# Three of eight 1/z factors brought to xT's layout by DMA, and a planner constant raised from 22 to 24

## The chip, the cores and the metric

The kernel runs on one core of one Trainium2 chip. The metric is the device time of one execution in microseconds, taken as the median of three runs. A core has five engines with queues of their own: TensorE (PE; its weight loads stand apart as PEld), VectorE (DVE), ScalarE (ACT), GpSimd (POOL) and SyncE (SP, which here only issues DMAs). Each works through its queue strictly in the order in which its instructions were written; a letter q behind an engine's name in a row means its sequencer, which issues DMAs and waits.

## The reference, cut to what matters

The program is masked attention followed by two feed-forward blocks. Only the attention's last line is touched by the change: each row of `attn` is divided by its own sum z.

```python
scores = np.where(mask, scale * np.matmul(q, k.transpose(0, 1, 3, 2)), -1e9)   # mask: equal 6-bit hash buckets
scores = scores - np.max(scores, axis=-1, keepdims=True)
attn = np.exp(scores)
attn = attn / (np.sum(attn, axis=-1, keepdims=True) + 1e-09)
attn_out = np.matmul(attn, v)                          # (2, 8, 768, 64)
x = attn_out.transpose(0, 2, 1, 3).reshape(2, 768, 512)
# gated block: h = relu(x @ w_in), spatial mixing by w_spatial, @ w_out
# second block: layer norm, relu(xn @ w_ch1) @ w_ch2, added to its input
```

## The kernel before

**Tiles.** There are 2 batches x 8 heads x 6 tiles of 128 queries, 96 tiles in all. A name such as `x_1_6_1_0` is tile x of batch 1, head 6, group 1 (of two groups of three tiles), tile 0 in the group. For each tile PE computes the scores `sc` (128 queries x 768 keys), DVE takes the masked minimum into `x`, ACT the exponential with its row sum into `z_sum`, PE turns `x` by 6 transposes into `pt` (PSUM, two halves), ACT and DVE copy the halves to `e`, and PE multiplies `e` by `vv` into `po`, once for each head. ACT and DVE copy `po` into `xT`, where a partition is a channel (64 channels for each of two heads of a pair) and a column is a query. `sc` has two PSUM buffers, and `pt`, `po`, `pm` and `pz` share a ring of four.

**Division by z.** The factors 1/z stand with queries on the partitions, `xT` has the queries in its columns. For each of the eight head pairs (`b`, `r`) `summed` adds 1e-9 and takes the reciprocal (`zr`, 128 x 12), one tile after the pair's last `weighted`; `normalized`, three tiles after it, lets POOL widen `zr` to 128 x 384 twice (`zw`), PE transpose each into PSUM (`pz`, three 128 x 128 transposes each), and DVE multiply `xT` by it in two halves. `attn_step` calls both.

**What comes after.** The gated block of batch 0 runs on PE between the tiles of batch 1's attention (`pv`, `pg`, `py`). Batch 1's own gated block begins when attention ends: `x_split` splits `xT` into high and low parts (`act_x`), and for it all four pairs of batch 1 must be divided. Then come the second block's matmuls (`pc`, `p`, `acc`). Weights come as 64-bit words (`f_v`, `f_u`, `f_w` in the rows, `f64_...` in the program) through ACT's DMA queue and are converted by ACT, DVE and POOL; the rest of the loads and all stores are issued by SP.

**What sets the order.** All calls are recorded as jobs. `Plan.run` gives each a start from its own table of costs and due times, twelve rounds of it are made, the best one by that table is kept, and the instructions of each engine are written in the order of these starts. A job that isn't PE's may not start more than `EARLY` before its due time `late[j]` (line 180 and `opened` in `run`), so `EARLY` moves work on every engine but PE directly, and on PE through what is ready:

```python
return max(when[i], bulk, late[j] - self.EARLY) if late and not j.soon else max(when[i], bulk)
```

Of the kernel before, what the change touches and what calls it, by code (L numbers as in the profile page):

```python
# [9 lines left out]
F32 = mybir.dt.float32  # L10
# [4 lines left out]
ALU = mybir.AluOpType  # L15
# [3 lines left out]
P = 128  # L19
# [150 lines left out]
class Plan:  # L170
# [6 lines left out]
    RUN = 6  # L177
    NEAR = 1.5
    LOOK = 55
    EARLY = 22.0  # L180
    BULK = 14.0
    ROUNDS = 12
    HOP = {"PE": 0.15, "ACT": 0.06, "DVE": 0.06, "POOL": 0.06, "SP": 0.05}
# [115 lines left out]
    def run(self, late=None):  # L299
# [20 lines left out]
        def opened(j):  # L320
# [3 lines left out]
            bulk = self.BULK if j.engine == "ACT" and j.bytes > 200000 else 0.0  # L324
            return max(when[i], bulk, late[j] - self.EARLY) if late and not j.soon else max(when[i], bulk)

# [185 lines left out]
def attn_moe_kernel(ctx: ExitStack, tc: tile.TileContext, qT, kT, v, proj, w_in, w_spT, b_sp, w_out, g_ln, w1, w2, out):  # L512
    fixed = ctx.enter_context(tc.tile_pool(name="fixed", bufs=1))
    ident = fixed.tile([P, P], F32, name="ident")
    make_identity(tc.nc, ident)
    nc = plan = Plan(tc)
    B, H, D, S = qT.shape
# [8 lines left out]
    NQT = S // P  # L526
# [25 lines left out]
    GW = GRP * P  # L552
    NG = NQT // GRP
    KC = S // 2
# [89 lines left out]
    dram = Pool(plan, "dram", space=bass.MemoryType.DRAM)  # L644
# [34 lines left out]
    xT = {}  # L679
    z_sum = {}  # L680

    pairs = {}
# [65 lines left out]
    NT = len(order)  # L748
# [74 lines left out]
    def head_prep3(b, h):  # L823
        vv = ap.tile([P, NKT, D], F32, tag="vv", name=f"vv_{b}_{h}", bufs=2)
        nc.sync.dma_start(out=vv, in_=v[b, :, h])
        heads[b, h]["vv"] = vv

    def group_prep(b, h, g):
        groups[b, h, g] = {"qs": passes_of("q", b, h, slice(g * GW, (g + 1) * GW))}

    def scores(b, h, g, j):
        jm = f"{b}_{h}_{g}_{j}"
        ks, qs = heads[b, h]["ks"], groups[b, h, g]["qs"]
        qsl = slice(j * P, (j + 1) * P)
        sc = ps_s.tile([P, 1024], F32, tag="sc", name=f"sc_{jm}")[:, :S]
        for csl in (slice(0, 512), slice(512, S)):
            for i, rows in enumerate((P, MR)):
                nc.tensor.matmul(
                    sc[:, csl], qs[:rows, i, qsl], ks[:rows, i, csl], start=(i == 0), stop=(i == 1)
                )  # L840
        tiles[b, h, g, j] = {"sc": sc}

    def masked_max(b, h, g, j):

        jm = f"{b}_{h}_{g}_{j}"
        t = tiles[b, h, g, j]
        x = ap.tile([P, S], F32, tag="x", name=f"x_{jm}", bufs=XB)
        nb = ap.tile([P, 1], F32, tag="nb", name=f"nb_{jm}", bufs=4)
        nc.vector.tensor_scalar(
            x,  # L850
            t["sc"],
            MASKED,
            FMAX,
            op0=ALU.min,
            op1=ALU.min,
            accum_out=nb,
        )
        t["x"], t["nb"], t["max"] = x, nb, plan.jobs[-1]
        if (b, h, g, j) == (0, 0, 0, 0):
            pair_split(0, 0, first=True)  # L860

    def exps(b, h, g, j):
        t, n = tiles[b, h, g, j], g * GRP + j
        nc.scalar.activation(
            t["x"], t["x"], AF.Exp, bias=t["nb"], scale=-1.0, accum_out=z_sum[b][:, n, h : h + 1]
        )

    def transposes(b, h, g, j):
        jm = f"{b}_{h}_{g}_{j}"
        t, gr = tiles[b, h, g, j], groups[b, h, g]  # L870
        if j == 0:
            gr["e"] = ap.tile([P, NKT, GW], F32, tag="e", name=f"e_{b}_{h}_{g}", bufs=EB)
        qsl = slice(j * P, (j + 1) * P)
        for c in range(2):
            pt = ps_b.tile([P, 3, P], F32, tag="b", name=f"pt_{jm}_{c}")
            for i in range(3):
                kt = c * 3 + i
                nc.tensor.transpose(pt[:, i, :], t["x"][:, kt * P : (kt + 1) * P], ident)
            e = gr["e"][:, c * 3 : c * 3 + 3, qsl]
            if c == 0 or (b == 0 and (g * GRP + j) % 2):  # L880
                nc.scalar.activation(e, pt, AF.Copy)
            else:
                nc.vector.tensor_copy(e, pt)

    def weighted(b, h):
        po = ps_b.tile([P, GW], F32, tag="b", name=f"po_{b}_{h}")
        for kt in range(NKT):
            for g in range(NG):
                nc.tensor.matmul(
                    po[g * D : (g + 1) * D],  # L890
                    heads[b, h]["vv"][:, kt],
                    groups[b, h, g]["e"][:, kt],
                    start=(kt == 0),
                    stop=(kt == NKT - 1),
                )
        own = slice(h % 2 * D, (h % 2 + 1) * D)
        nc.scalar.activation(xT[b][own, h // 2, 0:GW], po[0:D], AF.Copy)
        nc.vector.tensor_copy(xT[b][own, h // 2, GW:S], po[D:P])
        for g in range(NG):
            groups.pop((b, h, g))  # L900

    def summed(b, r):

        zr = ap.tile([P, NQT, 2], F32, tag="zr", name=f"zr_{b}_{r}")
        nc.vector.tensor_scalar(zr, z_sum[b][:, :, 2 * r : 2 * r + 2], 1e-9, None, op0=ALU.add)
        nc.vector.reciprocal(zr, zr)
        pairs[b, r]["zr"] = zr

    def normalized(b, r):

        zr = pairs[b, r]["zr"]
        for c in range(2):
            zw = ap.tile([P, 6, D], F32, tag="zw", name=f"zw_{b}_{r}_{c}", bufs=2)
            zc = zr[:, c * 3 : c * 3 + 3, :].rearrange("p a (h o) -> p (a h) o", o=1)
            nc.gpsimd.tensor_scalar(zw, zc.to_broadcast([P, 6, D]), 1.0, 0.0, op0=ALU.mult, op1=ALU.add)
            pz = ps_b.tile([P, 3, P], F32, tag="b", name=f"pz_{b}_{r}_{c}")
            for i in range(3):
                nc.tensor.transpose(pz[:, i, :], zw[:, 2 * i : 2 * i + 2].rearrange("p h d -> p (h d)"), ident)
            xs = xT[b][:, r, c * KC : (c + 1) * KC]
            nc.vector.tensor_tensor(xs, pz.rearrange("p a n -> p (a n)"), xs, op=ALU.mult)  # L920

    def attn_step(i):

        if 0 <= i < NT:
            transposes(*order[i])
        if 0 <= i + 2 < NT:
            b, h, g, j = order[i + 2]
            if (h, g, j) == (0, 0, 0):
                xT[b] = mp.tile([P, KFT, S], F32, tag="xT", name=f"xT_{b}")
                z_sum[b] = mp.tile([P, NQT, H], F32, tag="z_sum", name=f"z_sum_{b}")  # L930
            scores(*order[i + 2])
        if 0 <= i + 1 < NT:
            masked_max(*order[i + 1])
            exps(*order[i + 1])
        if 0 <= i - PO < NT and order[i - PO][2:] == (NG - 1, GRP - 1):
            weighted(*order[i - PO][:2])
        for late, e in ((1, summed), (3, normalized)):
            n = i - PO - late
            if 0 <= n < NT and order[n][1] % 2 == 1 and order[n][2:] == (NG - 1, GRP - 1):
                e(order[n][0], order[n][1] // 2)  # L940
        n = i + 1 + QA
        if GRP < n < NT and order[n][3] == 0:
            group_prep(*order[n][:3])
        n = i + NTH
        if NTH <= n < NT and order[n][2:] == (1, 0):
            head_prep3(*order[n][:2])
# [9 lines left out]
    for n0 in range(0, NT, 2 * NTH):  # L956
        b, h = order[n0][:2]
# [227 lines left out]
    ap = Pool(plan, "ap", 2, till=1)  # L1185
    conv0 = pools["conv"] = Pool(plan, "conv0", CB0, till=1)
    ps_s = Pool(plan, "ps_s", 2, space=PSUM, till=1)
    ps_b = Pool(plan, "ps_b", 4, space=PSUM, till=1)
# [18 lines left out]
    for n, f in enumerate(KEPT):  # L1207
        d = {}
# [21 lines left out]
    for i in range(-1 - QA, NT + PO + 3):  # L1230
        attn_step(i)
        for e in pair_steps.get(i, ()):
            e()
        if i == 2:
            nc.sync.dma_start(out=b_sb, in_=b_sp.rearrange("(n p) -> p n", p=P))
        plan.soon = True
        for e in conv_steps.get(i, ()):
            plan.behind = pools.get("abs", pairs[0, 1]["loaded"]) if e.__name__ in ("stage", "kept_stage") else None
            e()
        plan.soon, plan.behind = False, None  # L1240
        if i == M0:
            m0 = moe1(0, ps_b, "b")
        if m0 is not None:
            while n0 < (i - M0 + 1) * 24 / (NT - M0):
                next(m0, None)
                n0 += 1
# [362 lines left out]
    late = []  # L1609
    for n, (b, rs_of) in enumerate(runs):  # L1610
        for m, r in enumerate(rs_of):
# [25 lines left out]
            both = (2 * r, 2 * r + 1)  # L1637
# [43 lines left out]
```

## Time and profile before

| | |
|---|---|
| median of 3 runs | 646.39 us (645.65 to 646.80) |
| the profiled execution's own time | 645.79 us |
| its span, first to last instruction | 643.6 us |
| PE busy | 634.8 us, 99% of the span |
| DVE busy | 500.4 us, 78% |
| ACT busy | 327.7 us, 51% |
| POOL busy | 189.6 us, 29% |
| granted TensorE clock, mean | 0.999 of full speed |

Durations in the rows are of single instructions; on PE they overlap, so that a PE instruction's duration is longer than the distance to the next one's start. What an instruction takes out of PE's time is read from the chain of waits, which gives each piece only the time up to the next one.

### The profile page before, as it was taken

The numbers are of one execution on the slowest core, as the hardware profiler recorded it, in microseconds if no ns is written. First come the engines' busy times: TensorE is split into PE (matmuls) and PEld (weight loads), VectorE is DVE, ScalarE is ACT, GpSimd is POOL, SyncE is SP. The second block draws the span as 40 slices with busy tenths as digits, with TensorE's granted clock in tenths as the row PEclk, the third lists the DMA queues.
The fourth block names the chain that finished last, engine by engine and source line by source line (L and its number), as shares of the span: only waits on it lengthen the run. The fifth ranks groups of instructions, "written<-read, shape, count | busy, mean of one in ns | idle before, by whom it ended". The sixth has DMA issues, their size and how long they took to land.

```text
span 643.6 us, 10095 instructions
## 1 busy us (share of the span) xinstructions
PE 634.8 (99%) x3506; PEld 520.3 (81%) x3506; DVE 500.4 (78%) x998; ACT 327.7 (51%) x650; POOL 189.6 (29%) x186
## 2 busy tenths in 40 slices
PE   7999999999999999999999999999999999999997
PEld 5777767777787777877888888899999899898896
DVE  6789878797888686886799544699998887969555
ACT  7888877885565655643555323554323333333110
POOL 2142433244554633131343200122122324142200
PEclk9999999999999999999999999999999999999999
DMA  6776676667767877774653240421262626382623
GB/s 153 195 206 155 181 181 154 183 145 240 204 181 243 235 195 212 228 264 176 231 167 145 73 148 17 147 86 46 99 231 114 234 92 223 105 279 74 218 88 143
DMA packets 64738, 107.68 MB, mean 167 GB/s; under 512 B 7008, under 2 KB 33328, under 8 KB 64432
## 3 DMA queue, kind: packets, MB, share of 16 engines
q1 hardware_dynamic: 43232, 67.58, 36.0%
q10 hardware_dynamic: 21456, 39.46, 18.5%
q8 instruction: 28, 0.46, 0.3%
q14 instruction: 22, 0.18, 0.1%
HBM read 63.31 MB, written 24.90 MB: 137 GB/s over the span
## 4 chain that ended last, share of the span: by engine, by line
PE 94%; DMA 2%; DVE 2%; issue 1%; SPq 0%; POOL 0%; ACTq 0%; DVEq 0%; POOLq 0%
PE acc L502 20%; PE p L502 14%; PE pv L502 10%; PE sc L502 10%; PE pt L502 10%; PE po L502 9%; PE pg L502 7%; PE pc L502 5%; PE py L502 5%; DMA qs<-q 2%; PE pm L502 1%; PE pz L502 1%; PE ptr_g L502 1%; PE px_c L502 1%; DMA pj<-in_proj 1%
## 5 line engine op out<-in xcount | busy, mean ns | idle before, releaser
L502 PE MATMUL acc<-w,ch 128*128 128x512 f32 x576 | 142.9, 393 | 0.0
L502 PEld LDWEIGHTS acc<-w,ch 128*128 128x128 f32 x576 | 107.3, 188 | 18.9
L502 ACT ACTIVATE x<-x,nb 128x768 f32<-128x768 f32 x96 | 89.7, 936 | 31.3 <-DVE x L502 26.4
L502 DVE TENSOR_SCALAR_CACHE_REDUCE x<-sc 128x768 f32<-128x768 f32 x96 | 90.9, 951 | 6.8 <-PE sc L502 3.7
L502 PE MATMUL sc<-ks,qs 128*128 128x512 f32 (+3 forms) x384 | 93.8, 363 | 1.9 <-DVE x L502 1.2
L502 POOL TENSOR_TENSOR f64c_w<-f_w,f64c_w 128x512 f32<-128x512 f32 x32 | 44.1, 1380 | 152.9 <-issue 81.8
L502 PE MATMUL pt<-ident,x 128*128 128x128 f32 x576 | 81.3, 274 | 0.3 <-DVE xT L502 0.3
L502 PEld LDWEIGHTS pt<-ident,x 128*128 128x128 f32 x576 | 66.5, 140 | 14.9 <-issue 2.4
L502 PEld LDWEIGHTS sc<-ks,qs 128*128 128x128 f32 (+1 forms) x384 | 62.9, 190 | 13.9 <-issue 2.2
L502 PE MATMUL po<-e,vv 128*64 128x384 f32 x384 | 65.5, 490 | 0.0
L502 ACT ACTIVATE ch<-u 128x384 fp32r<-128x384 f32 x48 | 25.2, 525 | 79.1 <-DVE u L502 67.0
L502 ACT ACTIVATE e<-pt 128x384 f32<-128x384 f32 x120 | 55.0, 485 | 18.6 <-PE pt L502 18.1
L502 DVE TENSOR_TENSOR u<-p,u 128x384 f32<-128x384 f32 x84 | 45.4, 552 | 20.5 <-PE p L502 20.0
L502 PEld LDWEIGHTS po<-e,vv 128*64 128x64 f32 x384 | 26.1, 137 | 31.2 <-issue 29.8
L502 PE MATMUL p<-t,w 128*128 128x384 f32 x252 | 50.0, 337 | 0.0
L502 PE MATMUL p<-xh,w 128*128 128x384 f32 x252 | 48.8, 338 | 0.0
L502 DVE COPY e<-pt 128x384 f32<-128x384 f32 x72 | 39.7, 553 | 9.6 <-PE pt L502 9.0
L502 PEld LDWEIGHTS p<-t,w 128*128 128x128 f32 x252 | 44.9, 188 | 2.3
L502 PEld LDWEIGHTS p<-xh,w 128*128 128x128 f32 x252 | 44.6, 188 | 2.2 <-DVE u L502 0.3
L502 POOL TENSOR_TENSOR w<-f64c_w,w 128x512 fp32r<-128x512 f32 (+1 forms) x28 | 35.2, 1259 | 37.8 <-ACT w L502 15.0
L502 DVE TENSOR_SCALAR f64c_w<-f64c_w 128x512 f32<-128x512 f32 x64 | 30.8, 480 | 18.5 <-ACT f64c_w L502 15.8
L502 PE MATMUL pg<-vn,w_sp 128*128 128x512 f32 x180 | 43.6, 396 | 0.0
(155 smaller groups left out, 1018.5 us busy)
## 6 DMA issues: line engine op xcount, KB each, us to landing
f_w<-in_w ACTq DMA_DIRECT2D x32, 512.0 KB
ots<-y_dram SPq DMA_DIRECT2D x12, 768.0 KB
ks<-k SPq DMA_DIRECT2D x45, 192.0 KB
y_dram<-ots SPq DMA_DIRECT2D x30, 256.0 KB
qs<-q SPq DMA_DIRECT2D x30, 192.0 KB
wst_sp<-in_w_spT SPq DMA_DIRECT2D x12, 384.0 KB
vv<-in_v SPq DMA_DIRECT2D x16, 192.0 KB
qs<-q SPq DMA_DIRECT2D x30, 96.0 KB
```

The source lines that it names most:

```text
L502: res = getattr(getattr(nc, engine[j.engine]), op)(*map(live, args), **{k: live(x) for k, x in kw.items()})
```

## The change

Three pairs of batch 1 (`r` = 0, 1, 2) take another way. `zr` is laid out as 128 x (2 heads x 6 tiles), so that one transpose gives 12 rows of 128 queries (`pz`, 12 x 128); DVE copies these to `zt`, SP stores `zt` to `zd` in DRAM (6 KB), and two DMAs read it back, each row broadcast to 64 partitions, as `zb` (128 x 768). DVE multiplies `xT` by `zb` in one instruction. `normalized` for these pairs is called eight tiles behind, not three. The other five pairs keep PE's way; their `zw` is now one tile for both halves, in one buffer (shared with `zb`) where there were two, and POOL fills it with four instructions of 128 x 3 x 64 where there were two of 128 x 384. For all eight pairs the 1e-9 is added in two instructions (one for each head). `EARLY` goes from 22 to 24.

```diff
-    EARLY = 22.0
+    EARLY = 24.0
...
     def summed(b, r):
-        zr = ap.tile([P, NQT, 2], F32, tag="zr", name=f"zr_{b}_{r}")
-        nc.vector.tensor_scalar(zr, z_sum[b][:, :, 2 * r : 2 * r + 2], 1e-9, None, op0=ALU.add)
+        zr = ap.tile([P, 2, NQT], F32, tag="zr", name=f"zr_{b}_{r}")
+        for h in range(2):
+            nc.vector.tensor_scalar(zr[:, h], z_sum[b][:, :, 2 * r + h], 1e-9, None, op0=ALU.add)
         nc.vector.reciprocal(zr, zr)
         pairs[b, r]["zr"] = zr
+        if b == 0 or r == H // 2 - 1:
+            return
+        rows = 2 * NQT
+        pz = ps_b.tile([P, GW], F32, tag="b", name=f"pz_{b}_{r}")
+        nc.tensor.transpose(pz[:rows, :P], zr.rearrange("p h a -> p (h a)"), ident)
+        zt = ap.tile([rows, P], F32, tag="zt", name=f"zt_{b}_{r}", bufs=1)
+        nc.vector.tensor_copy(zt, pz[:rows, :P])
+        zd = dram.tile([2, 1, S], F32, tag=f"zd_{b}_{r}", name=f"zd_{b}_{r}")
+        nc.sync.dma_start(out=zd.rearrange("h o (a q) -> (h o a) q", a=NQT), in_=zt)
+        zb = ap.tile([P, S], F32, tag="zw", name=f"zb_{b}_{r}", bufs=1)
+        for h in range(2):
+            nc.sync.dma_start(out=zb[h * D : (h + 1) * D], in_=zd[h].to_broadcast([D, S]))
+        pairs[b, r]["zb"] = zb
     def normalized(b, r):
+        if "zb" in pairs[b, r]:
+            nc.vector.tensor_tensor(xT[b][:, r], pairs[b, r]["zb"], xT[b][:, r], op=ALU.mult)
+            return
         zr = pairs[b, r]["zr"]
+        both = ap.tile([P, S], F32, tag="zw", name=f"zw_{b}_{r}", bufs=1)
         for c in range(2):
-            zw = ap.tile([P, 6, D], F32, tag="zw", name=f"zw_{b}_{r}_{c}", bufs=2)
-            zc = zr[:, c * 3 : c * 3 + 3, :].rearrange("p a (h o) -> p (a h) o", o=1)
-            nc.gpsimd.tensor_scalar(zw, zc.to_broadcast([P, 6, D]), 1.0, 0.0, op0=ALU.mult, op1=ALU.add)
+            zw = both[:, c * KC : (c + 1) * KC].rearrange("p (a h d) -> p a h d", a=3, h=2)
+            for h in range(2):
+                zc = zr[:, h, c * 3 : c * 3 + 3].rearrange("p (a o) -> p a o", o=1)
+                nc.gpsimd.tensor_scalar(zw[:, :, h], zc.to_broadcast([P, 3, D]), 1.0, 0.0, op0=ALU.mult, op1=ALU.add)
...
-        for late, e in ((1, summed), (3, normalized)):
+        for late, e in ((1, summed), (3, normalized), (8, normalized)):
             n = i - PO - late
+            if late > 1 and (late == 8) != (n > NT // 2 and n < NT - 1):
+                continue
```

The order of the instructions changes in many places on each engine. Three of them matter below. The first is on PE, at the pair `r` = 1 of batch 1. Before, behind the first scores of head 5:

```order
L502 MATMUL pt_1_4_1_1_1_2707<-ident_58,x_1_4_1_1_2655 128x128 x3
L502 MATMUL sc_1_5_0_0_2711<-ks_1_5_0_2412,qs_1_5_0_2518 128x512 x2
L502 MATMUL sc_1_5_0_0_2711<-ks_1_5_0_2412,qs_1_5_0_2518 128x256 x2
L502 MATMUL pz_1_1_0_2719<-ident_58,zw_1_1_0_2613 128x128 x3
L502 MATMUL pz_1_1_1_2726<-ident_58,zw_1_1_1_2616 128x128 x3
L502 MATMUL pv_0_5_0_2731<-w_u_0_1170,act_x0_5_2424 128x512 x12
```

After, the pair's only transpose stands some ten rows earlier, between two tiles of head 4:

```order
L502 MATMUL pt_1_4_0_2_1_2636<-ident_58,x_1_4_0_2_2518 128x128 x3
L502 MATMUL sc_1_4_1_1_2640<-ks_1_4_0_2221,qs_1_4_384_2396 128x512 x2
L502 MATMUL sc_1_4_1_1_2640<-ks_1_4_0_2221,qs_1_4_384_2396 128x256 x2
L502 MATMUL pz_1_1_2650<-ident_58,zr_1_1_2528 12x128
L502 MATMUL pt_1_4_1_0_0_2652<-ident_58,x_1_4_1_0_2579 128x128 x3
L502 MATMUL pt_1_4_1_0_1_2658<-ident_58,x_1_4_1_0_2579 128x128 x3
```

Six transposes have become one; it reads `zr` itself, with no `zw` between. The second place is on ACT, in the first heads of batch 0, where the first piece of the weights (`f64_v_0`) is loaded and then read by `f64c_v_0`. Before:

```order
L502 ACTIVATE e_0_1_0_382<-pt_0_1_0_0_0_361 128x3x128
L502 DMA f64_v_0_387<-in_w_in 128x1024
L502 ACTIVATE x_0_1_0_2_377,z_sum_0_218<-x_0_1_0_2_377,nb_0_1_0_2_376 128x768
L502 ACTIVATE e_0_1_0_382<-pt_0_1_0_1_0_391 128x3x128
L502 ACTIVATE e_0_1_0_382<-pt_0_1_0_1_1_398 128x3x128
L502 ACTIVATE x_0_1_1_0_423,z_sum_0_218<-x_0_1_1_0_423,nb_0_1_1_0_422 128x768
L502 ACTIVATE x_0_1_1_1_431,z_sum_0_218<-x_0_1_1_1_431,nb_0_1_1_1_430 128x768
L502 ACTIVATE f64c_v_0_435<-f64_v_0_387 128x512
```

After:

```order
L502 ACTIVATE e_0_1_0_381<-pt_0_1_0_0_0_369 128x3x128
L502 ACTIVATE x_0_1_0_2_364,z_sum_0_215<-x_0_1_0_2_364,nb_0_1_0_2_363 128x768
L502 ACTIVATE e_0_1_0_381<-pt_0_1_0_1_0_389 128x3x128
L502 ACTIVATE e_0_1_0_381<-pt_0_1_0_1_1_393 128x3x128
L502 DMA f64_v_0_412<-in_w_in 128x1024
L502 ACTIVATE x_0_1_1_0_410,z_sum_0_215<-x_0_1_1_0_410,nb_0_1_1_0_409 128x768
L502 ACTIVATE x_0_1_1_1_430,z_sum_0_215<-x_0_1_1_1_430,nb_0_1_1_1_429 128x768
L502 ACTIVATE f64c_v_0_438<-f64_v_0_412 128x512
```

The load's issue has moved three instructions back, its reader has stayed in its place. The third place is near the end of attention, on SP, after the change (`wst_sp0_4` and `wst_sp0_5` are pieces of w_spatial, `qs_1_7_384` the queries of the last head's second group, `y_0_1` a result tile of batch 0):

```order
L502 DMA wst_sp0_4_3146<-in_w_spT 128x6x128
L502 DMA zb_1_0_3151<-zd_1_0_2321 64x768 x2
L502 DMA y_dram_3035<-y_0_1_3180 128x512
L502 DMA zb_1_1_3221<-zd_1_1_2897 64x768
L502 DMA qs_1_7_384_3236<-q2_1_3_2583 64x2x384
L502 DMA qs_1_7_384_3236<-q2_1_3_2583 64x384
L502 DMA qs_1_7_384_3236<-m_1_3_2786 12x384
L502 DMA zb_1_1_3221<-zd_1_1_2897 64x768
L502 DMA zd_1_2_3269<-zt_1_2_3214 12x128
L502 DMA wst_sp0_5_3302<-in_w_spT 128x6x128
L502 DMA zb_1_2_3322<-zd_1_2_3269 64x768 x2
```

and on DVE at the same place, where the first of these products stands ahead of the scores of head 6:

```order
L502 COPY e_1_6_0_3053<-pt_1_6_0_2_1_3182 128x3x128
L502 TENSOR_TENSOR xT_1_1862<-zb_1_0_3151,xT_1_1862 128x768
L502 COPY zt_1_2_3214<-pz_1_2_3196 12x128
L502 TENSOR_SCALAR x_1_6_1_1_3217,nb_1_6_1_1_3216<-sc_1_6_1_1_3186 128x768
L502 COPY e_1_6_1_3208<-pt_1_6_1_0_1_3204 128x3x128
L502 TENSOR_SCALAR x_1_6_1_2_3240,nb_1_6_1_2_3239<-sc_1_6_1_2_3210 128x768
```

The reads of `zb` stand late, close ahead of the products that take them, and all three pairs are divided within this stretch. `zb` has one buffer, so the read of `zb_1_1` waits for the product of `zb_1_0`, and `qs_1_7_384` stands behind it on SP.

## Rows read from the trace of the kernel before

**Rows 1.** The page's busy times: engine, us, share of the span, instructions.

```profile
PE 634.8 (99%) x3506; PEld 520.3 (81%) x3506; DVE 500.4 (78%) x998; ACT 327.7 (51%) x650; POOL 189.6 (29%) x186
```

**Rows 2.** What PE waited for: us in total, times, longest.

```profile
PE warm L502 <- POOL above L502: 1.4, 1, 1.4
PE pm L502 <- DVE qs L502: 1.3, 1, 1.3
PE sc L502 <- DVE x L502: 1.2, 2, 0.9
PE sc L502 <- DMA qs<-q: 0.5, 1, 0.5
PE pt L502 <- DVE xT L502: 0.3, 1, 0.3
PE sc L502 <- PE pt L502: 0.2, 1, 0.2
```

**Rows 3.** Windows, last stretch: length, then busy us of each engine, clock, DMA.

```profile
620.00:644.00 24.00, 19.82 (x93) 16.82 (x91) 12.76 (x22) 1.58 (x3) 0.00 (x0) 0.97 0.35 132
```

**Rows 4.** Instructions that touch pz: ns min/median/max, first and last start us.

```profile
L502 PE MATMUL pz<-ident,zw x48: 269/273/330, 46.6 to 302.6; 128*128 128x128 f32 x48
L502 DVE TENSOR_TENSOR xT<-pz,xT x16: 547/552/558, 47.9 to 303.7; 128x384 f32<-128x384 f32 x16
```

**Rows 5.** Chain of waits near the pair (1, 2): start us, us up to the next piece.

```profile
264.40 0.66 PE pz L502 x6
265.06 2.77 PE py L502 x12
```

**Rows 6.** Instructions that touch zw and zr: ns min/median/max, first and last start us.

```profile
L502 POOL TENSOR_SCALAR zw<-zr x16: 510/512/941, 36.3 to 294.6; 128x384 f32<-128x384 f32 x16
L502 DVE TENSOR_SCALAR zr<-z_sum x8: 161/169/1323, 34.1 to 293.6; 128x12 f32<-128x12 f32 x8
```

**Rows 7.** Timeline of DVE in the start: start us, us, [idle before].

```profile
9.49 0.55 DVE L502 SCALAR_TENSOR_TENSOR qs<-dup,qs 64x384 fp32r<-64x384 f32 x1 [0.88 <-ACT qs L502]
12.42 0.95 DVE L502 SCALAR_TENSOR_TENSOR k<-raws,k 128x768 fp32r<-128x768 f32 x1
15.91 0.55 DVE L502 COPY e<-pt 128x384 f32<-128x384 f32 x1
```

**Rows 8.** Timeline of ACT around the first weight load.

```profile
22.90 0.38 ACTq L502 DMA_DIRECT2D f_v<-in_w_in  x1
25.16 0.85 ACT L502 ACTIVATE e<-pt 128x384 f32<-128x384 f32 x2
...
28.87 0.69 ACT L502 ACTIVATE f64c_v<-f_v 128x512 f32<-128x512 f32 x1 [0.28 <-DMA f_v<-in_w_in]
...
30.80 0.49 ACT L502 ACTIVATE e<-pt 128x384 f32<-128x384 f32 x1 [0.74 <-PE pt L502]
...
32.80 0.94 ACT L502 ACTIVATE x<-x,nb 128x768 f32<-128x768 f32 x1 [0.48 <-DVE x L502]
```

**Rows 9.** Chain of waits: the two longest pieces that are DMAs of SP.

```profile
26.91 5.21 DMA qs<-q
218.18 5.33 DMA qs<-q
```

**Rows 10.** Timeline near the end of attention, SP, DVE, ACT and PE.

```profile
251.02 0.37 SPq L502 DMA_DIRECT2D wst_sp<-in_w_spT  x1
251.45 0.53 SPq L502 DMA_DIRECT2D vv<-in_v  x1
256.40 0.56 DVE L502 COPY e<-pt 128x384 f32<-128x384 f32 x1 [1.76 <-PE pt L502]
257.11 0.96 DVE L502 TENSOR_SCALAR_CACHE_REDUCE x<-sc 128x768 f32<-128x768 f32 x1
258.29 0.95 ACT L502 ACTIVATE x<-x,nb 128x768 f32<-128x768 f32 x1
262.87 0.81 PE L502 MATMUL pt<-ident,x 128*128 128x128 f32 x6
```

More of the change, by code (lines that the diff above doesn't have):

```diff
@@ L916, in normalized @@
             pz = ps_b.tile([P, 3, P], F32, tag="b", name=f"pz_{b}_{r}_{c}")
             for i in range(3):
-                nc.tensor.transpose(pz[:, i, :], zw[:, 2 * i : 2 * i + 2].rearrange("p h d -> p (h d)"), ident)
+                nc.tensor.transpose(pz[:, i, :], zw[:, i].rearrange("p h d -> p (h d)"), ident)
             xs = xT[b][:, r, c * KC : (c + 1) * KC]
```

## The prediction

> **What bounds the kernel now.** I read the busy times first. PE is busy in 634.8 of 643.6 us, the others are far below it (DVE 78%, ACT 51%, POOL 29%) [rows 1]. Busy time of a pipelined engine can hide slack, so next come the waits of PE. They sum to 4.9 us in seven places: 1.4 + 1.3 + 1.2 + 0.5 before 33 us, and only 0.3 + 0.2 in the 600 us that follow [rows 2]. The last window shows the rest: PE is busy 19.8 us from 620 on, and with the span's end at 643.6 some 3.8 us are the tail in which the last sums leave [rows 3]. 634.8 + 4.9 + 3.8 is the span to 0.1 us. So the kernel is PE's own work, end to end. A change is worth what it takes out of PE's queue, less what new waits it puts there; work moved between DVE, POOL and DMA counts only where PE then waits.
>
> **What leaves PE.** Three pairs give up six transposes each and get one: 18 go, 3 come, 15 net. What is one worth? Its row shows 273 ns from start to end [rows 4], but transposes overlap: the chain gives the six of pair (1, 2) 0.66 us until the next matmul goes on, 0.110 us each [rows 5]. The new one writes 12 rows and still passes 128 columns of the identity, so I give it the same 0.110; no trace shows a lone one of this shape. Its bounds are 0 and 0.273. So 18 x 0.110 = 1.98 go, 3 x 0.110 = 0.33 come, 1.65 us net (1.16 to 1.98 by the bounds). All of it lies on the path, since PE had no wait near these pairs [rows 2]. That the transposes stand in another place costs PE nothing: they need `zr`, which is older than the `zw` that they needed before.
>
> [...]
>
> **DVE.** Six products of 0.552 us [rows 4] go, three of 128 x 768 from SBUF come. Two-source instructions of that size take 0.95 [rows 7]: 3 x 0.95 = 2.85 against 3.31, so 0.46 less. Three copies 12 x 128 come, between the 0.17 of a 128 x 12 instruction [rows 6] and the 0.55 of a 128 x 384 copy [rows 7]; I take 0.2, 0.6 in all. Eight more additions at 0.17 are 1.4 [rows 6]. DVE gets about 1.5 us more in all (1.4 to 2.6), spread over 300 us in which it idles a fifth of the time [rows 1]: price 0. Without that cover it would be 2.6 at most.
>
> **POOL.** 16 instructions at 0.512 are 8.2 us; now 5 pairs x 4 at between 0.26 (half the columns) and 0.51 make 5.1 to 10.2 [rows 6]. POOL is idle 71% of the time [rows 1], and `pz` of batch 0 comes three tiles later: price 0.
>
> **The way through DRAM.** Per pair: one 6 KB store, two reads that write 192 KB each, on SP. The danger is not SP but DVE: it works in order, and the product of pair (1, 0) stands ahead of `x_1_6_1_1`. In the times of before: SP issues `wst_sp0_4` at 251.0 and is free at 251.4; each read then takes about the 0.53 of the load in that slot, so the second is issued by 252.5 [rows 10]. The longest landings on the chain are 5.2 and 5.3 us [rows 9]; that makes 257.8 at worst, while DVE comes free at 256.96 [rows 10]. Then 0.95 for the product and up to 0.55 for the `zt` copy behind it: `x_1_6_1_1` begins by 259.3 where it began at 257.11. Its exponential ended 2.13 us after its start (258.29 + 0.95) [rows 10], so now by 261.4; PE takes it at 262.87 [rows 10]. 1.4 us remain even at the long landing. The second pair's read waits for the first product, and behind it on SP stand the queries of the last head's second group, which PE takes only behind the three tiles of the first. Price 0; it turns into a wait if the landing takes more than 5.3 + 1.4 = 6.7 us.
>
> **EARLY and the order.** PE's own order moves by a few rows at a time, with the same instructions. What can change are the waits, at three places where before already waits:
> - The start, to about 19 us, bound by DVE. One 0.55 us instruction (`qs`) moves from ahead of the first `x` to behind the second, and the first copy of `e` (0.55) goes behind one more `x` (0.95) [rows 7]. A gain of at most 0.55, a loss of at most 0.95 where a transpose needs the PSUM buffer that this copy frees. DVE's total is the same: I take 0.
> - ACT's first weight load. Before it is issued at 22.90 and its reader starts at 28.87, having waited 0.28: a landing of 5.9 us under load [rows 8]. After, it is issued behind the second of two copies that begin at 25.16, so at about 25.6, 2.7 us later, with its reader in the same place. If the landing stays at 5.9, ACT stands until 31.5, and behind it are the `xT` copy, three `e` copies and an exponential. ACT's idle of 0.74 and 0.48 after it takes up 1.2 of the 2.7 [rows 8]; 1.5 is left at most. On the other side, the loads of the next scores then share the DMA engines less, and PE's 0.5 us wait for them (the one ended by `qs<-q`) [rows 2] can vanish. Ends -0.5 and +1.5; I take +0.3, nearer to no effect, since a later load shares less and lands sooner.
> - At 229 us PE waited 0.3 for DVE's copy of `po` [rows 2]; now a copy of `e` is written ahead of the conversion that made DVE late. -0.3 to 0, I take -0.3.
>
> **Sum.** -1.65 + 0 + 0.3 - 0.3 = -1.65 us. On the profiled execution: 645.79 - 1.65 = 644.1 (its span 643.6 to 642.0, the 2.2 us around it unchanged). The median of before lies 0.60 above this execution; on it the forecast is 646.39 - 1.65 = 644.7.
>
> **Rivals.**
> - *Given back by the order.* PE's saving is real, and ACT's late load or the start eats it. For it: PE's only waits stand exactly there, and the load moves without its reader. Against it: ACT has idle time behind it, and DVE's work in the start is the same. With the upper ends 1.5 and 0.95 it would be 647.2; with half of them 646.0. No measurable change.
> - *The division's round trip holds DVE* (slower). One place: `zb_1_0` at about 257. From 6.7 us of landing on, PE loses each further microsecond, since DVE stands and behind it the scores of head 6. To be slower by over 0.2% it takes 1.65 + 1.3 = 2.9 us more, 9.6 in all; at twice the longest landing shown, 10.7, the stall is 4.0 and the time 648.7. For it: the reads stand directly behind `wst_sp0_4`'s 384 KB in SP's queue, and a store to DRAM and a wait precede each. Against it: nothing on the chain lands as late [rows 9], and for the first pair the store is long past. [...]
> - *A transpose costs its whole duration.* Then 15 x 0.273 = 4.1 us go: 642.3. Against it stands the 0.66 for six [rows 5]. [...]
>
> **How the numbers follow.** About 0.2%, 1.3 us, is what a measurement of this kernel can tell from no change: below 645.1 is faster, above 647.7 slower. The forecast (net waits between -1.4, all three lower ends, and +0.35) has 0.47 and covers 643.3 to 645.1. Given back: 0.41, of which 0.03 beyond 647.7, if a wait comes that I don't see. The round trip: 0.09. The whole duration: 0.03. Faster 0.47 + 0.03 = 0.50, same 0.38, slower 0.12. The range 643.3 to 647.5 leaves out the round trip, the whole duration, and the ends of the two large cases, under 0.2 in all. The predicted time is that of the forecast, 644.7.
>
> **What will show it.** PE's busy time should fall by 1.5 to 2, and `pz` should have 33 matmuls where it had 48. The chain's pieces of the lone transposes should be 0.11 each; 0.25 would put the saving at 1.2. In PE's waits: no wait on `x` or `e` between 250 and 275 (else the round trip), and the sum of those before 40 us at 4.4 as before within 0.5 (else given back). DVE's idle before the three products `xT<-zb,xT` should be ended by DMA for under 1 us. ACT's idle before `f64c_v` at about 29 us tells the load's lateness: 0.3 before, up to 3 if the landing doesn't shorten. The forecast is wrong if PE waits over 0.4 us more than the 4.9 us of before.

## The result: slower, by waits at places that had none

The changed kernel takes 649.66 us (median of 5 runs, 648.96 to 652.36); the kernel before, run beside it, 645.81 (644.83 to 646.80). The ratio is 1.0068, with a 95% interval of 1.0046 to 1.0091: slower, and outside the range of the prediction. The profiled execution took 649.66 us, with a span of 647.9 (643.6 before).

The head of the page and the busy times of the kernel after (engine, us, share of the span, instructions), against [rows 1]:

```profile
span 647.9 us, 10087 instructions
PE 635.8 (98%) x3491; PEld 518.0 (80%) x3491; DVE 510.4 (79%) x1006; ACT 327.8 (51%) x650; POOL 190.6 (29%) x190
```

PE has its 15 instructions fewer, yet it is busy 1.0 us longer. What PE waited for, of the kernel after (us in total, times, longest), against [rows 2]:

```profile
PE sc L502 <- DMA qs<-m: 2.3, 1, 2.3
PE sc L502 <- DMA qs<-q: 2.2, 4, 1.0
PE warm L502 <- POOL above L502: 1.4, 1, 1.4
PE pt L502 <- ACT x L502: 0.5, 3, 0.2
PE acc L502 <- DVE ch L502: 0.5, 1, 0.5
PE p L502 <- DVE u L502: 0.5, 2, 0.3
PE sc L502 <- DVE x L502: 0.3, 1, 0.3
PE pm L502 <- ACT e L502: 0.2, 1, 0.2
```

They sum to 7.9 us where they were 4.9. The first two rows are loads for the scores, at 24, 37, 64, 92 and 136 us; `acc` and `p` stand in the second block, at 497 to 537 us. The kernel before had one wait for such a load, of 0.5 us at 32, and none in the second block.

7.9 - 4.9 explains 3.0 us, but the span grew by 4.3 with 1.65 less work. The rest hides in PE's busy time, since the ends of its matmuls are modelled and a short stall between two starts looks busy. So I use a measure of my own from here on. Each kind of matmul has a distance to the next start where nothing waits: 0.109 us for a transpose, 0.230 for 512 columns (0.228 in `acc`), 0.175 for 384, 0.120 for 256, 0.168 for a `po` matmul, 0.098 for `pm`. PE's work is the sum of these, 622.06 us before and 620.43 after. What a start lies behind the sum of all that stand ahead of it is lost time. In the profiled executions, one of each kernel, it is 17.75 us before and 23.73 after: 6.0 more lost less 1.6 of work is about 4.3, the growth of the span. It divides like this (us lost in each stretch):

| | to 40 us | 40 to 160 | 160 to 320 | 320 to end | sum |
|---|---|---|---|---|---|
| before | 8.7 | 4.7 | 3.2 | 1.2 | 17.75 |
| after | 9.2 | 9.1 | 2.1 | 3.3 | 23.73 |

That a lone transpose costs 0.11 is read from PE's timeline of the kernel after near the first of them (start us, duration us): 161.63 - 161.52.

```profile
160.74 0.94 PE L502 MATMUL sc<-ks,qs 128*128 128x512 f32 x4
161.52 0.27 PE L502 MATMUL pz<-ident,zr 128*12 128x128 f32 x1
161.63 0.82 PE L502 MATMUL pt<-ident,x 128*128 128x128 f32 x6
```

The instructions that touch `pz` in the kernel after (ns min/median/max, first and last start), against [rows 4]:

```profile
L502 PE MATMUL pz<-ident,zw x30: 270/272/328, 46.8 to 304.8; 128*128 128x128 f32 x30
...
L502 PE MATMUL pz<-ident,zr x3: 273/273/273, 161.5 to 259.6; 128*12 128x128 f32 x3
L502 DVE COPY zt<-pz x3: 272/273/274, 163.0 to 260.4; 12x128 f32<-12x128 f32 x3
```

And those that touch `zb`, with the idle time of DVE before them (what ended it: us, times):

```profile
L502 SPq DMA_DIRECT2D zb<-zd x6: 444/532/595, 252.1 to 270.9; - x6
L502 DVE TENSOR_TENSOR xT<-zb,xT x3: 948/959/1648, 259.5 to 276.5; 128x768 f32<-128x768 f32 x3
...
  DMA zb<-zd: 1.6, 2
```

The division does what it says: 33 transposes, and products before which DVE stands 1.6 us in all, with no wait of PE between 250 and 275.

**Where the new waits come from.** At 64 us PE waits for queries that SP issued at 58.68, where the kernel before issued them at 58.71 and did not wait. New is what ACT issues at 58.16: a weight load that stood at 50.8 before. ACT, SP and PE in the timeline of the kernel after (in brackets the idle time ahead, and what ended it):

```profile
58.16 0.34 ACTq L502 DMA_DIRECT2D f_v<-in_w_in  x1
...
58.68 1.34 SPq L502 DMA_DIRECT2D qs<-q  x2
...
64.10 0.70 PE L502 MATMUL sc<-ks,qs 128*128 128x512 f32 x2 [0.63 <-DMA qs<-q]
```

What the DMA queues moved from 59 to 62 us in the kernel after (packets, MB, share of the 16 engines; q1 is SP's, q10 is ACT's):

```profile
q10 hardware_dynamic: 144, 0.52, 66.9%
q1 hardware_dynamic: 114, 0.16, 22.0%
```

The same 3 us in the kernel before:

```profile
q1 hardware_dynamic: 277, 0.34, 53.0%
```

ACT's 512 KB take two thirds of the 16 engines' time (66.9%), and SP's queue moves half as much as before (0.16 MB against 0.34) and takes 22.0% of that time, where it took 53.0%. The wait at 92 us is alike (ACT's load at 85.8, at 79.9 before; from 87 to 90 us q10 moves 0.48 MB, before none). At 136 us it is SP that is late: the issue that feeds it takes 2.24 us where others of its kind take 0.79. SP and PE of the kernel after:

```profile
129.37 2.24 SPq L502 DMA_DIRECT2D qs<-m  x1
...
136.05 0.50 PE L502 MATMUL sc<-ks,qs 76*128 76x512 f32 x1 [2.30 <-DMA qs<-m]
```

In the second block it is a queue's order. ACT, DVE and PE in the timeline of the kernel after, ahead of PE's wait at 497 us:

```profile
488.16 0.63 ACT L502 ACTIVATE w<-f64c_w 128x512 fp32r<-128x512 f32 x1 [3.68 <-DMA f64c_w<-kept]
488.70 0.67 ACT L502 ACTIVATE f64c_w<-f_w 128x512 f32<-128x512 f32 x1
...
489.40 1.04 DVE L502 TENSOR_SCALAR f64c_w<-f64c_w 128x512 f32<-128x512 f32 x1 [3.07 <-ACT f64c_w L502]
...
496.26 0.43 DVE L502 TENSOR_TENSOR f_w<-f64c_w 128x256 f32<-128x256 f32 x1 [1.01 <-POOL f64c_w L502]
...
497.54 0.73 PE L502 MATMUL acc<-w,ch 128*128 128x512 f32 x2 [0.47 <-DVE ch L502]
```

The same two instructions on ACT in the kernel before:

```profile
483.87 0.66 ACT L502 ACTIVATE f64c_w<-f_w 128x512 f32<-128x512 f32 x1 [1.45 <-POOL w L502]
485.07 0.63 ACT L502 ACTIVATE w<-f64c_w 128x512 fp32r<-128x512 f32 x1 [0.55 <-DMA f64c_w<-kept]
```

Before, ACT converts the piece `f_w` first and then takes the load from `kept` (converted weights laid by in DRAM). After, the two stand the other way round: ACT waits 3.68 us for that load, and the conversion starts behind it. DVE's part of the conversion waits for ACT, POOL's begins at 494.91 where it began at 490.17 (the work around it runs only 2.4 us later than before), DVE waits for POOL, and `ch`, which `acc` needs, stands behind that on DVE (at 496.94). PE loses 0.8 us there. Its smaller waits at 505 and 537 us are not traced here.

### The profile page after: what moved, and what is told of

It reads as the page before. It is cut to its first block, busy times and chain, and to the rows that moved or that the text cites. A ratio compares the mean times of both kernels' runs of the same rounds, so it can differ in the third digit from the quotient of the medians.

```text
span 647.9 us, 10087 instructions
## 1 busy us (share of the span) xinstructions
PE 635.8 (98%) x3491; PEld 518.0 (80%) x3491; DVE 510.4 (79%) x1006; ACT 327.8 (51%) x650; POOL 190.6 (29%) x190
## 5 line engine op out<-in xcount | busy, mean ns | idle before, releaser
L502 DVE TENSOR_TENSOR u<-p,u 128x384 f32<-128x384 f32 x84 | 45.1, 549 | 14.5 <-PE p L502 13.8
L502 DVE TENSOR_SCALAR f64c_w<-f64c_w 128x512 f32<-128x512 f32 x64 | 36.2, 566 | 7.2 <-ACT f64c_w L502 7.0
```

Of the source, the lines that this page charges most:

```text
L502: res = getattr(getattr(nc, engine[j.engine]), op)(*map(live, args), **{k: live(x) for k, x in kw.items()})
```

## Experiments

Theories, as the expectations name them. A: EARLY = 24 itself makes operands late. B: the division's parts make the waits. C: neither does by itself; every newly planned order has its own small waits, and these differ by microseconds. D: EARLY acts in the second block. E: in the first, ACT's loads collide with those of the scores.

**The two parts alone, and other values of EARLY.** e1 is the kernel before with one number changed, e2 to e4 the changed kernel with another value there:

```
-    EARLY = 22.0
+    EARLY = 24.0
```

> The kernel before with EARLY = 24 and its division unchanged: the order alone. Where the 3.3 us came from is disputed; before the change the median is 645.8 in the latest comparison, after it 649.7 (ratio 1.0068). Theory A (an EARLY of 24 itself makes operands late: the splits of q and k on POOL behind the weights' conversions in the first batch, DVE behind a conversion in the second block): all of the loss stands here without the gain of 1.65, so 645.8 + 3.9 + 1.65 = 651.3, ratio 1.007 to 1.010, with PE waits of about 8 us, on qs<-q, qs<-m near 64, 92 and 136 us and on DVE's ch and u near 500. Theory B (the division's part of the change makes the waits): 645.5 to 646.3, PE's waits 4.5 to 5.5 as before. Theory C (no one part does: each newly planned order moves small waits, by some us either way): anything from 644 to 651, and not the sum's counterpart of the next run.

> The changed kernel with EARLY = 22 as before: the division alone. Theory A: 15 transposes less and no new waits: 645.8 - 1.65 = 644.2, ratio 0.997 to 0.998. Theory B: the waits of the changed kernel stay: 649 to 650, ratio 1.005 to 1.007. Theory C: 643 to 651, with new waits in PE at other places than in the changed kernel, and the two parts' differences (this run and the one before) do not add up to the 3.9 us of the whole change within 1 us.

> The changed kernel with EARLY = 20. Theory A: the lower EARLY the fewer late operands: 643.5 to 645, at most as long as with 22. Theory B: 649 to 650 as with 24. Theory C: no trend in EARLY: it differs from the run with 22 by over 1 us in either direction.

> The changed kernel with EARLY = 26. Theory A: more room, later operands: 650.5 to 653, above the 649.7 of 24. Theory B: 649 to 650. Theory C: no trend: it may well be below the run with 24.

The missing corners of the table, run later:

> The kernel before with EARLY = 20. Theory C: a new order, so 1 to 8 us longer than the 645.6 of the order with 22, in waits at other places; it does not stand 1.65 us above the changed kernel with EARLY = 20 (645.4). Theory A (EARLY sets the waits): with 20 fewer late operands than with 22: 644.5 to 646.

> The kernel before with EARLY = 26. Theory C: anything from 646 to 656, not ordered by EARLY (24 gave 656.2). Theory A: above the 656.2 of 24.

Medians, and the ratio to the kernel before with its interval:

| EARLY | division of before | new division |
|---|---|---|
| 20 | 644.98, 0.9995 (0.9985 to 1.0004) | 645.36, 0.9994 (0.9984 to 1.0005) |
| 22 | 645.6 (the kernel before) | 646.46, 1.0013 (1.0004 to 1.0022) |
| 24 | 656.19, 1.0148 (1.0131 to 1.0164) | 649.66, 1.0068 (the changed kernel) |
| 26 | 649.91, 1.0065 (1.0045 to 1.0086) | 648.93, 1.0047 (1.0035 to 1.0059) |

EARLY alone costs 10.6 us, the division alone 0.9, both together 4: the parts do not add up. e2 differs from the changed kernel in EARLY alone and is 3.2 us faster, so most of the loss came with the step of EARLY and not with the division. In neither column does the time rise with every step of EARLY (26 is faster than 24 in both), and at 24 the new division comes out 6.5 us faster than the old one. So A's figures fall (651.3 for e1, above 656.2 for b_early26), and so does B as the one cause. C fits the sums that do not add up, but it is not all: the four plans with 20 and 22 take 645.0 to 646.5 us, the four with 24 and 26 take 648.9 to 656.2, and for b_early20 C forecast 1 to 8 us more where A's 644.5 to 646 came out. In the profiles each of the four with 24 and 26 has a wait of PE of over 0.6 us for a load `qs<-q` between 60 and 110 us, and none of the four with 20 and 22. That a larger EARLY costs, if not in step with the number, is therefore not ruled out; eight plans do not decide it. Where e1 loses is told by PE's waits; the last two the changed kernel does not have:

```profile
PE sc L502 <- DMA qs<-q: 3.1, 3, 1.8
PE pt L502 <- ACT xT L502: 2.1, 1, 2.1
PE pt L502 <- DVE xT L502: 1.9, 1, 1.9
```

They stand at 222 and 237 us, and behind the second PE ran at half clock (0.50 from 240 to 242 us). e1's windows (length, busy us of PE, PEld, DVE, ACT and POOL, granted clock, DMA share, GB/s):

```profile
236.00:238.00 2.00, 1.01 (x7) 0.77 (x8) 1.94 (x5) 0.47 (x1) 0.00 (x0) 1.00 0.96 300
238.00:240.00 2.00, 2.00 (x11) 1.81 (x11) 2.00 (x6) 0.02 (x1) 1.30 (x1) 0.66 1.06 354
240.00:242.00 2.00, 2.00 (x6) 1.59 (x5) 0.76 (x2) 0.22 (x1) 0.00 (x0) 0.50 0.89 195
```

**The division in a fixed order.** Since each edit here makes a new plan, its own worth is seen only in an order that is kept. The next kernels plan the kernel before first, and give each instruction that both have the place it had there:

```
+    model = written(Plan(tc), ident, False, *arrays)
+    model.gates()
+    model.settle()
+    written(Plan(tc), ident, True, *arrays).issue(model)
```

> The new division written into the order of the kernel before: every instruction that both kernels have stands where it stood before (the order is taken from the plan of the kernel before), and only the new ones are put in. Theory C (the loss is the newly planned order, in many small waits, and the division itself is worth what PE loses of work): PE's waits stay near 5 us, the 1.65 us of 15 transposes come out of the span: 645.6 - 1.65 = 643.9, ratio 0.9965 to 0.998. Theory B (the division's own parts, the reads of zb and the halved zw instructions, make the waits): 646.5 to 649, with PE waits that the kernel before doesn't have.

> The counterpart: the division of before written into the order of the changed kernel. Theory C: the waits of the changed kernel (qs<-q at 64 and 92, qs<-m at 136, DVE's ch and u near 500) stay, and 15 transposes come back: 649.7 + 1.65 = 651.3, ratio 1.007 to 1.010. Theory B: without the reads of zb the waits go: 645.5 to 647.

f1 took 661.97 us (1.025, 1.0231 to 1.0269), f2 656.42 (1.0169, 1.0146 to 1.0191). f1 tells little of the division, for I set its instructions in badly: `zr` and `zw` came to stand behind other work than before, and PE waited 3.0 us in all for `zw`, 2.0 for ACT's copy of `xT` and 1.4 for `zr`. Behind the first two of these the clock was at half (0.50 of full speed) from 50 to 56 us and from 232 to 236. f2 is 6.8 us over the changed kernel, not 1.65: the old division set into that order has waits of its own, too. Both lie far from C's figures (643.9 and 651.3). The two show how far a few displaced rows go.

> Again the new division in the order of before, with its instructions set in with care: in f1 the additions for zr and the copies on POOL stood behind other work than before (PE waited 2.7 for zw at 49 and 1.4 for zr at 217). Here they stand where their counterparts stood, the lone transpose, its store, the reads and the products 1.5 to 5 us behind what they need by the plan, and nothing else is moved. Theory C (the division is worth PE's 1.65 us, the loss is the new order): 645.5 - 1.65 = 643.8, ratio 0.9965 to 0.9985, PE waits near 5 us. Theory B (the division's parts cost, however they are placed): 646 to 650, with waits at or behind the reads of zb between 190 and 300 us.

> The same, but set into the order that the plan of the kernel before takes with EARLY = 20 (645.0 without the new division). Theory C: 645.0 - 1.65 = 643.3, ratio 0.996 to 0.9975, faster than both kernels. Theory B: 645.5 to 650.

```
+            n = count[k[:3]] = count.get(k[:3], 0) + 1
+            like = loose.get((*k[:2], f"{k[2]}_{(n - 1) // 2}") if k[2].startswith("zw_") else k[:3])
+            if k[2][:3] in ("zr_", "zw_") and like:
+                j.start, j.end = like.start, like.end
...
+                j.start += {"pz_": 3.0, "zd_": 1.5, "zb_": 4.0, "xT_": 5.0}.get(to.base.name[:3], 0.0)
```

f3: 646.36 us (1.0027, 1.0009 to 1.0045); f4: 649.81 (1.0057, 1.0042 to 1.0071). In f3 PE had lost 14.13 us at 200 us, the kernel before 14.12: by these two profiles the changed forms in batch 0 cost nothing. From 200 to 240 it lost 2.1 more than before (the 2.6 in the next expectations is the sum of the two waits there and not the difference), at two `pt` that waited 1.2 at 216 and 1.3 at 230 for `xT`. Both runs miss what C forecast and lie within B's ranges. The next expectations put the wait at 230 down to ACT, which stood 3.2 us for a load of w_spatial (0.4 before). But that load was issued at 228.64, long behind the reads of `zb` (216; the changed kernel issues them at 252), and ACT's wait for it ended at 232.31, when the `pt` had already begun. What held the `pt` was DVE, as f3's timeline of DVE and PE shows:

```profile
226.85 0.95 DVE L568 TENSOR_TENSOR xT<-zb,xT 128x768 f32<-128x768 f32 x1
...
229.88 0.56 DVE L568 COPY xT<-po 64x384 f32<-64x384 f32 x1
...
230.50 0.55 PE L568 MATMUL pt<-ident,x 128*128 128x128 f32 x3 [1.31 <-DVE xT L568]
```

And DVE's copy in the kernel before:

```profile
228.85 0.56 DVE L502 COPY xT<-po 64x384 f32<-64x384 f32 x1
```

The product waited for no read. It stands in DVE's queue ahead of the copy that the `pt` takes and costs 0.95 us there; the copy begins 1.03 us later. In f4 the product at this place took 2.62 us. PE's wait is 3.2 us there, at 232, and the clock falls behind it: 0.70 from 232 to 234 us, 0.50 from 234 to 236.

The reads, and with them the products, moved behind `wst_sp0_4`, where the changed kernel has them:

> As f3, but the reads of zb stand on SP behind the load wst_sp0_4, where the changed kernel has them, and the products on DVE likewise; nothing else is moved. In f3 PE lost as much as before up to 200 us (14.1 in both) and 2.6 us more than before between 200 and 240, where the first reads of zb stood behind a load of wst_sp and ACT waited 3.2 for that load (0.4 before). Theory C with this cause: the 2.6 us go, PE's waits on xT at 216 and 230 with them, 645.7 - 1.65 = 644.0, ratio 0.9965 to 0.9985. If the division costs at any place (theory B): 645.5 to 647, with new waits between 250 and 290.

> The same in the order that the kernel before takes with EARLY = 20 (645.0 by itself, 649.8 with the reads in the place of f3, where PE waited 3.2 for xT at 232 and ran at half clock behind it). Theory C: 645.0 - 1.65 = 643.3, ratio 0.9955 to 0.9975, the wait at 232 and the low clock gone. Theory B: 645 to 648.

```
+                if to.base.name[:3] == "zb_":
+                    j.start = max(j.start, behind)
```

(`behind` is 0.6 us after the start of `wst_sp0_4`; the offsets for `zb_` and `xT_` are 1.0 and 4.0 now.)

f5: 645.40 us (0.9998, 0.9987 to 1.0008), with 1.7 us less lost from 200 to 240 us than f3, and no wait at 230. f6: 648.81 (1.0049, 1.0034 to 1.0063), its wait at 231 still 2.6 us: no read and no product stands near it now, so their place was not its cause there, and that cause stays open. f6 is 3.8 us over b_early20, whose order it keeps. In that order the division costs, which B says and C does not; it is also more than either theory's figure. f5 is the cleanest trial of the division: everything else where it was, and a mean granted clock of 0.999 in its profile. It comes out 0.35 us faster than before, which is no difference by its interval, not 1.65; the interval leaves room for no more than 0.85. Two of PE's waits in its profile give back what PE saved:

```profile
PE pt L574 <- ACT xT L574: 1.1, 1, 1.1
PE pg L574 <- DVE e L574: 0.8, 1, 0.8
```

The first of them in the timeline of f5, on ACT and PE:

```profile
215.42 0.66 ACT L574 ACTIVATE f64c_w<-f_w 128x512 f32<-128x512 f32 x1 [1.97 <-DMA f_w<-in_w]
...
215.99 0.58 ACT L574 ACTIVATE xT<-pv 128x512 f32<-128x512 f32 x1
...
216.62 0.55 PE L574 MATMUL pt<-ident,x 128*128 128x128 f32 x3 [1.12 <-ACT xT L574]
```

The transposes ahead of this `pt` began at 213.20, in the kernel before at 214.33: PE was 1.1 us early, what the ten transposes less of two pairs give (10 x 0.109). The conversion on ACT began at 215.42, where it had begun at 214.90. Its weight load was issued 0.7 us earlier than before (208.77, 209.49) and yet came 0.5 us later; why, is not shown. So `pt` starts at 216.62 as it had at 216.56.

**EARLY in the second block.**

> The changed kernel with EARLY = 24 for the first part (attention and first block) and 22 for the second block. By the traces the changed kernel lost 2.0 us more than before between 480 and 560 us, where PE waits for DVE's ch and u. Theory D (there EARLY itself is the cause: the conversions of the weights come to stand later or behind a load issued later): 649.7 - 1 to 2 = 647.7 to 648.7, the waits on ch and u go, those at 64, 92 and 136 stay. Theory C without D: 649 to 651, other waits of the same size there.

> The kernel before with EARLY = 24 in the second block alone (from the first instruction of that part on, at about 320 us; all ahead of it stands as before). Theory D (in the second block EARLY itself makes DVE late): PE loses 2 us more between 480 and 560 us, as the changed kernel (2.6 there, 0.5 before) and the run with EARLY = 24 alone (2.8) did: 645.7 + 2.0 = 647.7, ratio 1.002 to 1.004, waits on ch or u near 500. Theory C without D (only a newly planned order, either sign): 645 to 647, the stretch within 1 us of before.

```
-            return max(when[i], bulk, late[j] - self.EARLY) if late and not j.soon else max(when[i], bulk)
+            return max(when[i], bulk, late[j] - (24.0 if j.part else self.EARLY)) if late and not j.soon else max(when[i], bulk)
```

(g3, on the kernel before; g1 has 22.0 there, on the changed one.) g1 lost 0.7 us between 480 and 560 where the changed kernel lost 2.6, as D expects, and its median is 648.67 (1.0050, 1.0029 to 1.0072; the interval overlaps the changed kernel's). ACT's two instructions near 485 us stand there as in the kernel before. But g3 lost 0.7 as well, against 0.5 before, and took 645.52 (1.0000, 0.9990 to 1.0009), though on its ACT the two stand as in the changed kernel:

```profile
483.54 0.63 ACT L502 ACTIVATE w<-f64c_w 128x512 fp32r<-128x512 f32 x1 [2.46 <-DMA f64c_w<-kept]
484.08 0.65 ACT L502 ACTIVATE f64c_w<-f_w 128x512 f32<-128x512 f32 x1
```

With 2.46 us of waiting for the load instead of 3.68 no wait of PE followed. So D falls as it stands: 24 in the second block turned the two round and did no harm by itself. In the changed kernel it did, where the load took 1.2 us longer; what the new first part has to do with that is not shown.

**Two loads moved.**

> The changed kernel in its own order, with only two of ACT's 512 KB weight loads moved behind four to five more ACT instructions (the fourth of f_v, issued at 58.2 in the changed kernel where it was 50.8 before, and the first of f_out, 131.0 where it was 129.2). Theory E (the scores' waits at 64 and 136 come from these loads: their packets run at 59 to 62 and 132 to 135.4, just when the small qs loads that PE needs next are under way): PE's wait of 0.6 at 64 goes and that of 2.3 at 136 falls by 1 us or more; the time falls by 1 to 2.5 us, to 647.2 to 648.7, unless waits come elsewhere. Rival (the splits on POOL are late, or SP is): both waits stay within 0.3 us, the time within 0.7 of 649.7.

```
+LATER = {"f64_v_3": 4.0, "f64_out_0": 4.0}
```

g2 took 650.49 us (1.0076, 1.0053 to 1.0099), no gain where E forecast 1 to 2.5 us. Of the waits of PE that the profile puts down to loads of the scores only one is left, at 39 us:

```profile
PE sc L563 <- DMA qs<-q: 1.5, 1, 1.5
```

Those at 64 and 136 are gone. For the wait at 64 that speaks for E: the changed kernel, g1 and f2, in which the load stands where it stood, have it (0.6, 0.7 and 0.5 us). For the one at 136 it does not: g1, whose first part is that of the changed kernel, starts the same load in the same place and has no wait there. What is seen to differ in g1 is the issue on SP, which took 2.24 us in the changed kernel:

```profile
130.75 0.79 SPq L502 DMA_DIRECT2D qs<-m  x1
```

The wait at 92, whose load was not moved, stays (0.8 at 93; the profile names DVE, which ended just before). Others came (0.3 at 145 and 0.5 at 146), and by 20 us, ahead of any moved instruction, g2 had lost 1.3 us more than the changed kernel's profile. Executions of one order differ, too: at 38 us g1 waited 2.1 us where the changed kernel waited 0.3. So E is borne out for the wait at 64, not for the one at 136 and not for the time.

Lost time in the profiled executions of all of them (us, stretches as above):

| | to 40 us | 40 to 160 | 160 to 320 | 320 to end | sum |
|---|---|---|---|---|---|
| e1 | 10.4 | 6.8 | 8.7 | 3.6 | 29.55 |
| e2 | 8.3 | 8.4 | 2.6 | 2.5 | 21.78 |
| e3 | 8.8 | 6.1 | 2.6 | 1.3 | 18.87 |
| e4 | 9.0 | 6.9 | 3.7 | 3.4 | 23.04 |
| b_early20 | 8.5 | 4.9 | 2.9 | 0.9 | 17.25 |
| b_early26 | 7.9 | 6.8 | 2.4 | 2.5 | 19.59 |
| f1 | 9.2 | 13.8 | 11.9 | 1.7 | 36.54 |
| f2 | 9.8 | 10.9 | 2.6 | 3.4 | 26.69 |
| f3 | 9.0 | 4.5 | 5.2 | 1.2 | 19.86 |
| f4 | 9.4 | 4.8 | 8.3 | 1.8 | 24.29 |
| f5 | 9.4 | 4.3 | 4.5 | 1.5 | 19.69 |
| f6 | 8.8 | 5.1 | 9.4 | 1.1 | 24.41 |
| g1 | 10.3 | 6.8 | 2.1 | 1.4 | 20.58 |
| g2 | 11.3 | 7.6 | 2.1 | 3.1 | 24.14 |
| g3 | 8.9 | 4.0 | 2.3 | 1.3 | 16.51 |

No kernel beat the kernel before by more than its interval: the best, b_early20, e3, f5 and g3, end between 645.0 and 645.5.

## Why the prediction was wrong

**What leaves PE: the size right, "all of it lies on the path" wrong.** 15 transposes at 0.109 are 1.6 us, and the lone ones cost 0.11 as taken. But that PE had no wait near the pairs did not put the saving on the path. In the kept order of f5 0.35 of it came out at the end, which noise alone could make, and in its profile the waits at 216 and 286 took what was missing: at 216 PE, 1.1 us early, stood still for a weight load that came no earlier. In the kept order of f6 the division cost 3.8 us. Part of the difference may be the start, where f5's execution had lost 1.0 us more by 20 us than f3's in the same order.

**DVE, POOL and the way through DRAM: right for the changed kernel.** A product took 0.96 (0.95 forecast), the copy 0.27 (0.2), POOL's halves 0.35, inside the bounds. The reads cost DVE 1.6 us, more than the "under 1 us" of the text, and PE nothing. The rival of the round trip did not happen in the changed kernel. Nor did it in f3, where the reads come early: DVE waited for none of them, and what PE lost at 230 was the product's own 0.95 us ahead of a copy, a cost that the prediction looked for in one place only.

**EARLY and the order: this step failed.** It said that "PE's own order moves by a few rows at a time" and "what can change are the waits, at three places where before already waits". At the three places it was near:
- The start lost 7.0 us by 20 us in both, as forecast.
- ACT's first load was issued at 25.27 (25.6 forecast), and its reader began 4.78 us later (5.97 before), with ACT waiting 1.51 for it; PE lost 0.5 more by 40 us (0.3 forecast).
- The wait at 229 us went.

But 6.6 us came in where the kernel before had next to no wait to show, 4.4 between 40 and 160 us and 2.2 behind 320 (1.1 less was lost between 160 and 320). The step took the list of waits for the list of places with little slack. A place with 0.1 us of slack and one with 5 look alike there. Rows moved on ACT, not PE's, decided at 64 us, and by the same signs at 92, when a 512 KB load started and beside what, and at 497 us which conversion stood behind a load; the wait at 136 came with one long issue on SP. I followed one such load, the first, and did not ask the same of the others, which the same change had moved (the fourth by 7.4 us, the sixth by 5.9).

**The nearest rival** was "given back by the order", which named the mechanism and stopped at 647.2, since it summed the ends of the same three places. That one number re-plans the whole kernel had no chance of its own.

**The signs to look for.** By its own last line the prediction is wrong: PE waited 3.0 us more, where 0.4 was the limit. The sum of waits before 40 us was a poor sign. It fell from 4.4 to under 3 while the lost time rose by 0.5: waits split into stalls too short to be listed.

## What to carry to other kernels

Where a planner writes the order, an edit is two changes: what it does, and a new plan. Here eight plans, which differ by one number and the division, lie between 645.0 and 656.2 us, and a step of 2 in that number was worth up to 10.6 us, so the spread of plans belongs into the range before any term of the sum. Measure the edit itself in a kept order, better in two (here it came to -0.35 us in one and 3.8 in the other), and then ask at each saving what PE meets next there: behind a load that comes no earlier, a saving is waited away.

## What the runs showed of the hardware

PE's granted clock fell to 0.50 of full speed behind some waits and not behind others: behind 1.9 us in e1 (0.50 from 240 to 242 us), 2.0 in f1 (0.50 from 232 to 236) and 3.2 in f4 (0.50 from 234 to 236). Behind the 2.6 us of f6 it was between 0.8 and 0.9 in the mean of the profile's slice from 227 to 243 us. It stayed at 1.00 behind the 2.3 us of the changed kernel (136 to 140 us) and 2.1 us each in e1 (222 to 232) and g1 (38 to 48). Of f3's eleven executions six with a mean granted clock of 0.999 or 1.000 took 645.4 to 646.4 us, the five at 0.995 to 0.997 took 647.8 to 651.9. So a wait of PE was followed by matmuls at 0.50 in e1, f1 and f4, and in f3 the longer executions of one and the same order have the lower mean clock. This is not the only scatter: two executions of g1, both at 1.000, took 646.5 and 649.9 us.

Some long issues on SP stand beside packets of the queue that the trace calls instruction (28 packets, 0.46 MB in the changed kernel, 16 KB each). In the changed kernel all five issues of over 1.5 us before 200 us (at 74.3, 93.5, 109.0, 129.4 and 190.3; issues of the same kinds take 0.5 to 0.8) lie within 0.2 us of the start of such a packet, as this one in the window from 129.2 to 131.8:

```profile
q8 instruction: 1, 0.02, 4.4%
```

The five issues took 0.9 to 1.5 us more than others of their kinds. The other five such packets in these 200 us met no issue that long, and two issues behind 200 us (1.57 us at 240.0, 1.75 at 247.3) have no packet beside them, so the two do not always go together. The places differ between the kernels: in the kernel before, the three longest issues up to 200 us stand at 92.0, 126.5 and 186.2 (1.52, 1.45 and 2.08 us).
